# First expert products over 240 token columns instead of 256

## The chip, the core and the metric

The kernel runs on one core of a Trainium2 chip. The metric is the device time of one launch in microseconds (us), taken as the median of several runs. The engines of the core are named as the profile names them: PE is the matrix engine (PEld its weight loads), DVE the vector engine, ACT the scalar engine, POOL the GpSimd engine, and SP issues most transfers.

## What is computed

Three layers follow each other. A linear attention with a decaying state gives 3072 rows `x` of 384 numbers. A first layer of eight experts sends each row that a skip score lets through to one expert and adds the gated result. A second layer mixes all rows into 32 slots, four for each of eight other experts, and spreads the outcome over the rows again. The change lies in the first expert layer:

```
for e in range(8):
    mask = e_idx == e
    h = np.maximum(xc[mask] @ w1[e], 0.0)          # w1[e]: 384 x 1024
    y[mask] = gate_w[mask, None] * (h @ w2[e])     # w2[e]: 1024 x 384
out[do_compute] = xc + y
```

How many rows an expert gets depends on the data. For the inputs that `setup_inputs` draws with seed 0 the fullest expert has 205 rows; with seeds 1 to 7 the fullest has 240.

## The kernel before

The rows of one expert are gathered into a block with room for `CAP = 256` tokens, two halves of 128. Places that no token takes hold zeros or are masked later. `gload(e)` fetches the block from DRAM by an index list on POOL, `gtr(e, ...)` turns it on PE, and ACT and DVE write it as a rounded high part and a rounded rest, `xh` and `xl` (tile `xhl` in the profile), 128 x 3 x 256 each. The matrix products of this layer are made in the rounded four-byte type `F32R`; to keep four-byte accuracy each product is three: high by high, low by high, high by low.

The layer is a loop over `n` from 0 to 31, four steps for each expert; one step takes 256 of the 1024 inner features. In one step stand, in this order:

- `mm1(n)`: the first product, with weights as the stationary side (128 x 128 pieces of `wa`) and tokens as the moving side, 256 columns. There are six pieces (three of the 384 inputs by two of the features) and three products for each, so 18 products a step: L1251, L1252 and L1254, all into the PSUM tile `hp`.
- `split`: ACT rounds the next pieces of weights (L1007) and DVE makes their rests (L995).
- `act(n)`: ACT takes the positive part of `hp` into `hh` (L1261), and DVE makes the rest `hlo` (L1262). Both tiles are 128 x 2 x 256, two buffers each, taken anew from a pool in every step.
- `mm2(n-1)`: the second product of the step before, with 128 tokens of `hh` or `hlo` as the stationary side and 384 columns of weights as the moving side: 12 products, L1276 to L1278, into `yp`.
- between these, pieces of the work around the experts: `fin_a` adds the gated outcome to the rows (L1284 on DVE), `fin_b` to `fin_d` make the logits of the second layer, `gtr` turns the block of the next expert, `wload` fetches weights three half experts ahead (L957, L959), and `vload` fetches weights of the second layer (L200).

The order of PE, DVE, ACT and POOL is written out by hand: they run the program in the order of the code. SP follows the same order in this part; at the end of the program stands a read of the flag `bad` into a register on every engine (L1587), and on SP the scheduler puts that read where it likes after the flag is written.

The flag is written in step `n == 2` by four small DVE operations (L1383 to L1388) out of the counts of rows. Where an expert has more than 256 rows, a second program, `general`, computes everything again after the fast one. After the loop come the second layer's experts (`experts`: L214, L223, L232) and the mixing into the output (`combine`: L297 to L304).

Of the kernel before, what the change touches and what calls it, by code (L numbers as in the profile page):

```python
# [8 lines left out]
F32 = mybir.dt.float32  # L9
F32R = mybir.dt.float32r  # L10
BF16 = mybir.dt.bfloat16
I32 = mybir.dt.int32
AF = mybir.ActivationFunctionType
ALU = mybir.AluOpType
# [5 lines left out]
P = 128  # L20
# [3 lines left out]
E = 8  # L24
F = 1024
CAP = 256
XW = DM + 1
NOROW = 65536
NEG = -1.0e30
# [442 lines left out]
def tile_main(ctx, tc, rk, kv, wu, wcat, phi, w1, w2, v1, v2, r_in, k_in, v_in, w_in, u_in, wcn, out, dbg=None, force=False):  # L472
    nc = tc.nc
# [79 lines left out]
    cn = {"ident": ident, "onesf": onesf, "sel4": sel4, "w8": w8}  # L553
    x = xp.tile([P, NT, XW], F32, name="x")
    tj_i = kp.tile([P, 2, NT], I32, name="tj_i")
# [32 lines left out]
    n = 1  # L588
# [175 lines left out]
    tok8 = ry.tile([P, 2 * B, 16], BF16, tag="tok8", bufs=1, name="tok8")  # L764
    hot8 = ry.tile([P, 2 * B, CAP], BF16, tag="hot8", bufs=1, name="hot8")
    ipl = ry.tile([P, CAP], F32, tag="ipl", bufs=1, name="ipl")
    selb = rt.tile([P, E], BF16, tag="selb", bufs=1, name="selb")
# [14 lines left out]
    def hots(g, bs, eng):  # L782

        j0, nb = GR[g]
        if g < 4 and g not in HOT:
            HOT[g] = hot8[:, B:] if g % 2 else ry.tile([P, B, CAP], BF16, tag="hot", bufs=1, name=f"hot{g}")
        for b in bs:
# [3 lines left out]
    def gathered(g):  # L791

        li = ps.tile([P, CAP], F32, tag="t", name=f"lip{g}")
        for b in range(B):
            nc.tensor.matmul(li[32 * b : 32 * b + 32, :], tok[g % 2][:, b, :], HOT[g][:, b, :], start=True, stop=True)
        LI.append(ry.tile([P, CAP], BF16, tag="li", name=f"li{g}"))
        nc.scalar.copy(LI[g], li)
# [216 lines left out]
    if True:  # L1014
        for i in range(NT):
# [89 lines left out]
            if i == 4:  # L1105
# [6 lines left out]
                nc.vector.tensor_sub(tj[:, 1], tf[:, 1], tj[:, 0])  # L1112
                nc.gpsimd.iota(ipl.bitcast(I32), pattern=[[E, CAP]], base=-NOROW, channel_multiplier=0)
                nc.gpsimd.tensor_copy(ipl, ipl.bitcast(I32))
# [14 lines left out]
        fs = rt.tile([P, E], BF16, tag="fs", bufs=1, name="fs")  # L1129
# [39 lines left out]
        hl = fst.enter_context(tc.tile_pool(name="hl", bufs=1))  # L1169
        cw = hst.enter_context(tc.tile_pool(name="cw", bufs=2))  # L1170
# [10 lines left out]
        def gates_of(e):  # L1181
            for bl in range(2):
                fetched(XT[e][3][:, bl : bl + 1], g_d, e, bl)

        def fetched(o, src, e, bl):
            nc.gpsimd.indirect_dma_start(  # L1186
                out=o, out_offset=None, in_=src,
                in_offset=bass.IndirectOffsetOnAxis(ap=idg[:, bl, e : e + 1], axis=0),
                bounds_check=B * S - 1, oob_is_err=False,
            )  # L1190
# [4 lines left out]
        nc.vector.scalar_tensor_tensor(ltm[:, 16:24, :], m8.to_broadcast([P, 8, 32]), NEG, lg8[:, :, 9:41], op0=ALU.mult, op1=ALU.add)  # L1195
        nc.vector.tensor_reduce(cmax2, ltm[:, 16:24, :].rearrange("t b s -> t s b"), axis=AX.X, op=ALU.max)
        nc.gpsimd.tensor_copy(lt[:, 16:24, :], lg8[:, :, 9:41])
        gates_of(0)
        gates_of(1)
        gv = Group("v", cmax2, ltm[:, 16:24, :], 8, lambda j: x[:, 16 + j], lx[:, 1:2, :], mcs[:, 1:2])  # L1200
# [43 lines left out]
    def mm1(n):  # L1244
        xh, xl = XT[n // 4][1:3]
        hi, lo = WS.pop(("a", n))
        hp = pc.tile([P, 2, CAP], F32, tag="hp", name=f"hp{n}")

        fk = [(f, k, slice(f * P, f * P + P)) for k in range(3) for f in range(2)]
        for f, k, fs in fk:  # L1250
            nc.tensor.matmul(hp[:, f, :], hi[:, k, fs], xh[:, k, :], start=(k == 0 and f == 0), stop=False)  # L1251
            nc.tensor.matmul(hp[:, f, :], lo[:, k, fs], xh[:, k, :], start=False, stop=False)  # L1252
        for f, k, fs in fk:
            nc.tensor.matmul(hp[:, f, :], hi[:, k, fs], xl[:, k, :], start=False, stop=(k == 2 and f == 1))  # L1254
        HH[n] = [hp]

    def act(n):
        hp = HH[n][0]
        hh = cw.tile([P, 2, CAP], F32R, tag="hh", bufs=2, name=f"hh{n}")
        hlo = cw.tile([P, 2, CAP], F32R, tag="hlo", bufs=2, name=f"hlo{n}")  # L1260
        nc.scalar.activation(hh, hp, AF.Relu)  # L1261
        nc.vector.scalar_tensor_tensor(hlo, hp, 0.0, hh.bitcast(F32), op0=ALU.max, op1=ALU.subtract)  # L1262
        HH[n] = (hh, hlo)

    def mm2(n):
# [74 lines left out]
    if True:  # L1340
# [4 lines left out]
        for n in range(NS + 1):  # L1345
# [5 lines left out]
            if n < NS:  # L1351
                mm1(n)
                if 1 < n + 1 < NS and n > 0:
                    split("a", n + 1)
                if n > 1:
                    split("b", n)
                act(n)
            f = e - 1
# [22 lines left out]
            if n == 2:  # L1381
                mxc = mk.tile([P, 1], F32, name="mxc")
                nc.vector.tensor_reduce(mxc, cnt[:, 0:E].rearrange("p e o -> p (e o)"), axis=AX.X, op=ALU.max)  # L1383
                okc = mk.tile([P, 1], F32, name="okc")
                nc.vector.tensor_scalar(okc, mxc, float(E * CAP), None, op0=ALU.is_le)
                okw = mk.tile([P, 1], F32, name="okw")
                nc.vector.scalar_tensor_tensor(okw, cnt[:, E, :], float(E * PR), okc, op0=ALU.is_equal, op1=ALU.mult)
                nc.vector.tensor_scalar(bad, okw[0:1], -1.0, 1.0, op0=ALU.mult, op1=ALU.add)  # L1388
# [38 lines left out]
            if n == 23:  # L1427
                for i, o in enumerate((0, 1536)):
                    k = next(vit)
                    V[k] = vload(nc, XV, f"xv{i}", 1, k, v1, v2)  # L1430
            if n == 4:
                k = next(vit)
# [7 lines left out]
            if n % 2 == 1 and 3 <= n < 3 + 2 * NVX:  # L1440
                k = next(vit)
                V[k] = vload(nc, vx, "vx", NVX, k, v1, v2)
            if n % 2 == 1 and n // 2 + 3 >= 2 * E:
                for _ in range(2 if n < NS - 1 else 1):
                    k = next(vit)
# [49 lines left out]
        nm = mk2.tile([32, 1], F32, name="nm")  # L1495
# [159 lines left out]
```

## Time and profile before

| | us |
|---|---|
| median of three runs | 358.16 |
| the three runs | 357.42, 358.16, 359.10 |
| the profiled execution | 355.71 |
| its span, first to last instruction | 354.0 |

| engine | busy us | share of the span |
|---|---|---|
| PE | 326.0 | 92% |
| PEld | 261.7 | 74% |
| DVE | 230.9 | 65% |
| ACT | 160.8 | 45% |
| POOL | 141.7 | 40% |

The busy time of PE adds the whole length of products that overlap in its pipeline, with modelled ends, so a busy PE is not a PE at its peak. What one product costs in a dense row is read from the distance between two starts, and what an engine loses from the rows on waiting. The chain of work that ended last holds a single row in this profile (the read of the flag on ACT) and tells nothing here, so the stages are read one by one.

### The profile page before, as it was taken

What the parts mean: (1) busy time and instruction counts of PE and PEld (TensorE: products, weight loads), DVE (VectorE), ACT (ScalarE), POOL (GpSimd) and SP (SyncE); (2) the same over time, 40 slices, a digit from 0 to 9 for tenths busy, and PEclk for the clock granted to TensorE, in tenths of its full rate; (3) what the DMA queues carried; (4) which work ended last, traced back from release to release, by engine and by line L of the source; (5) the groups of instructions that cost most, each with busy time, mean ns of one, the idle gap of its engine ahead of it and who ended that gap; (6) DMA issues with size and microseconds to landing.
All of it is one profiled execution on the core that took longest, in us unless ns stands there. A gap on an engine that the chain in (4) does not pass through costs nothing. (4 is left out here: it accounts for less than half of the span.)

```text
span 354.0 us, 10396 instructions
## 1 busy us (share of the span) xinstructions
PE 326.0 (92%) x4316; PEld 261.7 (74%) x4316; DVE 230.9 (65%) x510; ACT 160.8 (45%) x351; POOL 141.7 (40%) x179
## 2 busy tenths in 40 slices
PE   8888998899798998999999999999999999999750
PEld 3556775777676683999999999998999998734340
DVE  6658678786878737776674847665575846417650
ACT  2234553445344554554655546554654643221360
POOL 4737775676655564814323242525224102200000
PEclk9999999999999999999999999999999999999985
DMA  7956568576678955789788787778856639489396
GB/s 243 312 166 187 148 196 277 176 215 190 201 214 277 386 211 182 269 269 317 263 275 284 241 266 258 252 271 270 306 179 224 221 107 329 156 270 372 119 328 214
DMA packets 45735, 85.29 MB, mean 241 GB/s; under 512 B 3838, under 2 KB 26672, under 8 KB 45680
## 3 DMA queue, kind: packets, MB, share of 16 engines
q1 hardware_dynamic: 43024, 80.63, 68.5%
q0 software_dynamic: 2128, 3.74, 3.7%
q8 instruction: 36, 0.59, 0.7%
q10 hardware_dynamic: 528, 0.16, 0.2%
q14 instruction: 19, 0.16, 0.2%
HBM read 74.49 MB, written 10.10 MB: 239 GB/s over the span
## 5 line engine op out<-in xcount | busy, mean ns | idle before, releaser
L1251 PE MATMUL hp<-xhl,wa 128*128 128x256 f32 x192 | 48.5, 289 | 0.2 <-ACT xhl L1241 0.2
L1252 PE MATMUL hp<-xhl,wa 128*128 128x256 f32 x192 | 47.1, 282 | 0.0
L1276 PE MATMUL yp<-wb,hh 128*128 128x384 f32 x128 | 45.1, 352 | 0.0
L995 DVE TENSOR_TENSOR wa<-w,wa 128x768 fp32r<-128x768 f32 x32 | 30.5, 956 | 22.0 <-ACT wa L1007 22.0
L1278 PE MATMUL yp<-wb,hlo 128*128 128x384 f32 x128 | 42.9, 335 | 0.0
L1277 PE MATMUL yp<-wb,hh 128*128 128x384 f32 x128 | 42.8, 335 | 0.0
L629 POOL TENSOR_TENSOR pd<-rkb 112x512 f32<-112x512 f32 x24 | 30.6, 1273 | 27.8 <-PE ud L657 23.4
L1186 POOL DMA_INDIRECT xg<-x_d,idg x16 | 19.9, 1242 | 52.1 <-DVE x L1284 39.4
L1306 POOL DMA_INDIRECT lt_d<-lsr,ids x16 | 17.7, 1106 | 52.5 <-ACT xhl L1241 29.9
L1251 PEld LDWEIGHTS hp<-xhl,wa 128*128 128x128 f32 x192 | 36.4, 190 | 0.5 <-ACT xhl L1241 0.5
L1252 PEld LDWEIGHTS hp<-xhl,wa 128*128 128x128 f32 x192 | 36.5, 190 | 0.0
L744 PE MATMUL yp<-at,kvt 64*48 64x64 f32 (+3 forms) x800 | 26.4, 248 | 7.2 <-DVE at L705 6.8
L995 DVE TENSOR_TENSOR wb<-w,wb 128x768 fp32r<-128x768 f32 x32 | 30.6, 955 | 2.4 <-ACT wb L1007 2.2
L744 PEld LDWEIGHTS yp<-at,kvt 64*48 64x48 f32 (+1 forms) x800 | 20.0, 120 | 15.0 <-DVE at L705 9.6
L705 DVE COPY_PREDICATED at<-ih,ud 128x512 f32<-128x512 int32 x24 | 17.4, 726 | 20.8 <-ACT us L686 8.7
L1261 ACT ACTIVATE hh<-hp 128x512 fp32r<-128x512 f32 x32 | 19.1, 598 | 26.0 <-PE hp L1254 26.0
L1007 ACT CAST wb<-w 128x768 fp32r<-128x768 f32 x32 | 26.8, 837 | 8.8 <-PE yp L1278 5.0
L1262 DVE SCALAR_TENSOR_TENSOR hlo<-hp,hh 128x512 fp32r<-128x512 f32 x32 | 22.0, 688 | 12.4 <-ACT hh L1261 12.4
L1254 PE MATMUL hp<-xhl,wa 128*128 128x256 f32 x192 | 28.2, 283 | 0.0
L1007 ACT CAST wa<-w 128x768 fp32r<-128x768 f32 x32 | 26.9, 840 | 0.0
L1276 PEld LDWEIGHTS yp<-wb,hh 128*128 128x128 f32 x128 | 24.1, 188 | 3.5 <-issue 3.5
L1254 PEld LDWEIGHTS hp<-xhl,wa 128*128 128x128 f32 x192 | 25.3, 192 | 0.0
(344 smaller groups left out, 693.3 us busy)
## 6 DMA issues: line engine op xcount, KB each, us to landing
w<-in_w_dram SPq DMA_DIRECT2D x32, 768.0 KB, 5.5
v<-in_v_dram SPq DMA_DIRECT2D x29, 768.0 KB, 6.8
rkb<-in_rk_dram SPq DMA_DIRECT2D x24, 448.0 KB, 5.6
kvt<-in_kv_dram SPq DMA_DIRECT2D x24, 384.0 KB, 3.7
x_d<-x SPq DMA_DIRECT2D x5, 768.0 KB, 6.5
out_dram<-ob SPq DMA_DIRECT2D x5, 768.0 KB, 6.8
x<-in_v_dram SPq DMA_DIRECT2D x2, 768.0 KB, 5.9
x_d<-x SPq DMA_DIRECT2D x2, 384.0 KB, 2.9
```

The lines of the kernel that those rows point to most:

```text
L629: nc.gpsimd.tensor_mul(t["pd"], rkt[:, 0], rkt[:, 1])
L744: nc.tensor.matmul(d, kvt[s0 : s0 + HT, 1, h * D : h * D + m], w, start=(c == ph == z == 0), stop=(ph == z == 1))
L995: nc.vector.tensor_sub(lv, sl, hv.bitcast(F32))
L1007: nc.scalar.copy(hv, sl)
L1186: nc.gpsimd.indirect_dma_start(out=o, out_offset=None, in_=src, in_offset=bass.IndirectOffsetOnAxis(ap=idg[:, bl, e : e + 1], axis=0), bou ...
L1251: nc.tensor.matmul(hp[:, f, :], hi[:, k, fs], xh[:, k, :], start=(k == 0 and f == 0), stop=False)
L1252: nc.tensor.matmul(hp[:, f, :], lo[:, k, fs], xh[:, k, :], start=False, stop=False)
L1254: nc.tensor.matmul(hp[:, f, :], hi[:, k, fs], xl[:, k, :], start=False, stop=(k == 2 and f == 1))
L1262: nc.vector.scalar_tensor_tensor(hlo, hp, 0.0, hh.bitcast(F32), op0=ALU.max, op1=ALU.subtract)
L1276: nc.tensor.matmul(YP[e][bl], hh[:, f, bs], hi[:, f, :], start=st, stop=False)
L1277: nc.tensor.matmul(YP[e][bl], hh[:, f, bs], lo[:, f, :], start=False, stop=False)
L1278: nc.tensor.matmul(YP[e][bl], hlo[:, f, bs], hi[:, f, :], start=False, stop=en)
```

## The change

`mm1` streams 240 token columns instead of 256, and writes 240 of the 256 columns of `hp`. `act` reads and writes 2 x 240 columns instead of 2 x 256. `hh` and its rest (now `hl`) are no longer taken anew from a pool in every step: two fixed pairs are made ahead of the loop, used in turn, and the last 16 columns of each half are set to zero once by four operations on POOL. `mm2` is unchanged; it reads all 256 columns, and so takes the zeros. The flag now asks for more than 240 rows.

```diff
+ROOM = 240
...
         nc.gpsimd.tensor_copy(lt[:, 16:24, :], lg8[:, :, 9:41])
+        HB = [[cw.tile([P, 2, CAP], F32R, tag=f"h{nm}{i}", bufs=1, name=f"h{nm}{i}") for nm in "hl"] for i in range(2)]
+        for ts in HB:
+            for t in ts:
+                nc.gpsimd.memset(t[:, :, ROOM:CAP].bitcast(F32), 0.0)
         gates_of(0)
         gates_of(1)
...
-            nc.tensor.matmul(hp[:, f, :], hi[:, k, fs], xh[:, k, :], start=(k == 0 and f == 0), stop=False)
-            nc.tensor.matmul(hp[:, f, :], lo[:, k, fs], xh[:, k, :], start=False, stop=False)
+            nc.tensor.matmul(hp[:, f, 0:ROOM], hi[:, k, fs], xh[:, k, 0:ROOM], start=(k == 0 and f == 0), stop=False)
+            nc.tensor.matmul(hp[:, f, 0:ROOM], lo[:, k, fs], xh[:, k, 0:ROOM], start=False, stop=False)
         for f, k, fs in fk:
-            nc.tensor.matmul(hp[:, f, :], hi[:, k, fs], xl[:, k, :], start=False, stop=(k == 2 and f == 1))
+            nc.tensor.matmul(hp[:, f, 0:ROOM], hi[:, k, fs], xl[:, k, 0:ROOM], start=False, stop=(k == 2 and f == 1))
...
-        hh = cw.tile([P, 2, CAP], F32R, tag="hh", bufs=2, name=f"hh{n}")
-        hlo = cw.tile([P, 2, CAP], F32R, tag="hlo", bufs=2, name=f"hlo{n}")
-        nc.scalar.activation(hh, hp, AF.Relu)
-        nc.vector.scalar_tensor_tensor(hlo, hp, 0.0, hh.bitcast(F32), op0=ALU.max, op1=ALU.subtract)
+        hh, hlo = HB[n % 2]
+        h, l, p = (t[:, :, 0:ROOM] for t in (hh, hlo, hp))
+        nc.scalar.activation(h, p, AF.Relu)
+        nc.vector.scalar_tensor_tensor(l, p, 0.0, h.bitcast(F32), op0=ALU.max, op1=ALU.subtract)
...
-                nc.vector.tensor_scalar(okc, mxc, float(E * CAP), None, op0=ALU.is_le)
+                nc.vector.tensor_scalar(okc, mxc, float(E * ROOM), None, op0=ALU.is_le)
```

PE has the same number of rows in the same order before and after; the 576 products of `mm1` have another width. POOL has four rows more, ahead of the fetches of the gates of the first two experts. Before, on POOL, between the fetch of the first two blocks (`xg`) and the step that clears a column of the rows (`x`):

```order
L1186 DMA xg_2688<-x_d,idg 128x384 x2
L1197 COPY ltt<-lg_213 128x256
L1186 DMA gg_2680<-g_d,idg 128x1 x2
L1186 DMA gg_2689<-g_d,idg 128x1 x2
L1342 MEMSET x_2767 128x16
```

The same place after; `hh` and `hl` are the two fixed pairs:

```order
L1187 DMA xg_2688<-x_d,idg 128x384 x2
L1198 COPY ltt<-lg_213 128x256
L1202 MEMSET hh_2708 128x2x16
L1202 MEMSET hl_2709 128x2x16
L1202 MEMSET hh_2710 128x2x16
L1202 MEMSET hl_2711 128x2x16
L1187 DMA gg_2680<-g_d,idg 128x1 x2
L1187 DMA gg_2689<-g_d,idg 128x1 x2
L1347 MEMSET x_2775 128x16
```

So four fetches of gates stand behind four clearings. In `mm2` of the first two steps, the products that read the second half of `hh` and `hl` now wait for POOL; no other wait on PE, DVE or ACT in the loop is new.

On SP one thing moved. Before, at steps 4 to 7 (`w` and `v` are weights of the two layers):

```order
L200 DMA ltt<-in_v_dram 128x3x512
L957 DMA w_2_1_3118<-in_w_dram 128x3x512
L959 DMA w_2_1_3120<-in_w_dram 128x4x384
L200 DMA v_2_0_3122<-in_v_dram 128x3x512
L1587 TENSOR_LOAD bad
L1587 ISA x2
L957 DMA w_3_0_3240<-in_w_dram 128x3x512
```

After:

```order
L201 DMA ltt<-in_v_dram 128x3x512
L1592 TENSOR_LOAD bad
L1592 ISA x2
L958 DMA w_2_1_3114<-in_w_dram 128x3x512
L960 DMA w_2_1_3116<-in_w_dram 128x4x384
L201 DMA v_2_0_3118<-in_v_dram 128x3x512
L958 DMA w_3_0_3232<-in_w_dram 128x3x512
```

The read of the flag, which waits for DVE, went ahead of three transfers.

## Rows read from the trace of the kernel before

**Rows 1.** Busy time by stretch: us, then PE, PEld, DVE, ACT, POOL, clock, DMA.

```profile
162.00:301.00 139.00, 139.00 (x1017) 132.17 (x1016) 90.12 (x155) 73.35 (x142) 43.10 (x38) 1.00 0.76 253
```

**Rows 2.** Who waited for whom, 162 to 301 us: total, times, longest.

```profile
DVE wa L995 <- ACT wa L1007: 21.7, 14, 3.3
ACT hh L1261 <- PE hp L1254: 20.3, 26, 1.3
```

**Rows 3.** Timeline of PE in two steps: start us, length us, product.

```profile
236.24 0.28 PE L1251 MATMUL hp<-xhl,wa 128*128 128x256 f32 x1
...
237.67 0.88 PE L1254 MATMUL hp<-xhl,wa 128*128 128x256 f32 x6
...
239.02 0.33 PE L1276 MATMUL yp<-wb,hh 128*128 128x384 f32 x1
...
240.41 0.34 PE L1278 MATMUL yp<-wb,hlo 128*128 128x384 f32 x1
```

**Rows 4.** Products by line and shape, whole run: count, then busy us, mean ns.

```profile
L1251 PE MATMUL hp<-xhl,wa 128*128 128x256 f32 x192 | 48.5, 289 | 0.2 <-ACT xhl L1241 0.2
L1254 PE MATMUL hp<-xhl,wa 128*128 128x256 f32 x192 | 28.2, 283 | 0.0
L1277 PE MATMUL yp<-wb,hh 128*128 128x384 f32 x128 | 42.8, 335 | 0.0
L1298 PE MATMUL lgq<-x2t,ph 128*32 128x256 f32 x42 | 4.4, 391 | 0.0
L214 PE MATMUL ehp<-v,spx 128*32 128x512 f32 x78 | 10.9, 595 | 0.0
L1536 PE MATMUL s<-l,onesf 128*128 128x32 f32 x4 | 0.6, 276 | 0.0
```

**Rows 5.** Timeline of PE behind the loop: four narrow products in a row.

```profile
307.09 0.61 PE L1536 MATMUL s<-l,onesf 128*128 128x32 f32 x4
```

**Rows 6.** ACT and DVE, 162 to 301 us, by line and shape.

```profile
L1262 DVE SCALAR_TENSOR_TENSOR hlo<-hp,hh 128x512 fp32r<-128x512 f32 x28 | 19.2, 687 | 9.8 <-ACT hh L1261 9.8
L1242 DVE TENSOR_TENSOR xhl<-xtp,xhl 128x256 fp32r<-128x256 f32 x18 | 7.0, 418 | 1.1 <-ACT xhl L1241 0.7
L1261 ACT ACTIVATE hh<-hp 128x512 fp32r<-128x512 f32 x27 | 16.1, 598 | 20.3 <-PE hp L1254 20.3
L1241 ACT CAST xhl<-xtp 128x256 fp32r<-128x256 f32 x18 | 6.1, 379 | 0.0
```

**Rows 7.** Timelines of POOL, PE and DVE, start of the loop.

```profile
142.81 0.42 POOL L1197 COPY ltt<-lg 128x256 f32<-128x256 f32 x1
...
148.71 0.14 POOL L1342 MEMSET x<- 128x16 f32 x1
...
148.48 0.33 PE L1276 MATMUL yp<-wb,hh 128*128 128x384 f32 x1
...
162.50 1.20 DVE L1284 SCALAR_TENSOR_TENSOR x<-yp,gg,xg 128x384 f32<-128x384 f32 x2
```

**Rows 8.** Timelines of DVE and SP around the flag, and its read on SP (ns).

```profile
153.67 0.14 DVE L1388 TENSOR_SCALAR bad<-okw 1x1 int32<-1x1 f32 x1
...
152.11 0.48 SPq L200 DMA_DIRECT2D ltt<-in_v_dram  x1
157.16 0.37 SPq L957 DMA_DIRECT2D w<-in_w_dram  x1
...
L1587 SPq TENSOR_LOAD <-bad x1: 473/473/473, 160.7 to 160.7; - x1
```

**Rows 9.** Behind the loop: SP's last weight transfers, PE's wait, DMA by stretch.

```profile
310.43 10.34 SPq L200 DMA_DIRECT2D v<-in_v_dram  x8
...
332.46 0.85 PE L232 MATMUL sop<-v,x 128*32 128x384 f32 x8 [0.58 <-DMA v<-in_v_dram]
...
303.00:310.00 7.00, 7.00 (x60) 4.90 (x62) 2.31 (x13) 1.44 (x5) 2.36 (x3) 1.00 0.26 86
311.00:331.00 20.00, 20.00 (x204) 7.74 (x200) 10.97 (x27) 4.43 (x9) 0.59 (x1) 1.00 0.97 334
...
SPq L200 <- PE ehp L214: 12.3, 3, 10.6
```

## The prediction

> **What bounds the kernel now.** I first cut the span into stages and looked at the one that the change touches, the loop over the experts, from about 143 to 301 us; the row is its main part. In it PE has work in flight all the time, at a granted clock of 1.00, which is the 2.4 GHz level, while DVE is busy 90.12 of 139 us, ACT 73.35 and POOL 43.10, and the DMA engines 0.76 of the time [rows 1]. Second, the waits of that stretch: PE heads none of them. ACT waits 20.3 us in 26 pieces for the last product of `mm1`, and DVE waits 21.7 us for ACT [rows 2]. So the loop is as long as PE's queue of products, and what the change takes from PE there is taken from the loop. Third, since a busy PE counts overlapping products whole, I took the price of a product from the distances between starts [rows 3]. The twelve products from 236.24 to 237.67 are 1.43 us apart, 119 ns each; the six that follow take 0.88 us, and less the 283 ns of the last one [rows 4] that is 0.60 us for five, again 119 ns. The eight 384-column products from 239.02 to 240.41 stand 174 ns apart.
>
> **Part 1, 16 columns less in 576 products.** One hundred twenty-eight columns more cost 174 - 119 = 55 ns, or 0.43 ns a column. The mean lengths say the same in another way: 335 ns at 384 columns against 283 at 256 [rows 4], 0.41 ns a column. That is one column a cycle of the 2.4 GHz level. I take 0.41, so 16 columns are worth 6.6 ns. At 256 columns 256 x 0.41 = 105 ns of the 119 are columns, and some 13 ns come on top; at 384 columns the rest is 174 - 157 = 17 ns. So the distance at 240 columns should be 119 - 6.6 = 112 ns. The count is 3 x 192 = 576, of which [rows 4] shows two of the three lines (the middle one has as many): 576 x 6.6 ns = **3.8 us**.
>
> A product cannot follow another faster than its weights are loaded. Each of these products has its own 128 x 128 weights. The trace has a row of narrow products with weights of that size: four of 32 columns take 0.61 us in all [rows 5], the last 276 ns long [rows 4], so three distances fill 0.334 us, 111 ns each, although 32 columns at the 0.80 ns a column of plain f32 (worked out below) would fill only 26 ns. I read 111 ns as the floor that the weight load sets. The 112 ns that I expect lie just above it, so the floor should not bite; it would at some 238 columns. Because the first product of each of the 32 rows of 18 waits for something else and because the floor is so near, I take **3.6 us** from the 3.8. The bounds are 576 x (119 - 111) = 4.6 us, and nothing, if the 13 ns come on top of the floor too (a rival, below).
>
> The Trainium skill (TensorE: Matmul & The Clock Gate, sections "LDWEIGHTS" and "Back-to-back issue gap") puts a load of 128 columns at 107 ns and a product at its columns over 2.4 GHz plus 2.5 ns. By that the distance would be 109 ns at 256 columns and then the load's 107, a gain of 2.5 ns a product and 1.4 us in all. The measured 119 and 111 ns [rows 3 to 5] are both higher than the page's, and the gap between them is three times as wide, so the sum above goes by the rows.
>
> **Part 2, ACT and DVE.** `act` has 32 columns less on each. ACT takes 598 ns for 512 columns and 379 for 256, 0.86 ns a column; DVE 687 and 418, 1.05 [rows 6]. So 27 and 34 ns a step, 0.9 and 1.1 us in all. Both wait for PE in the loop [rows 2], so I count nothing. The two blocks are no longer contiguous; were that to cost more than it saves, the 20 us of ACT's waiting would cover it, and without that cover 100 ns more a step would be 3.2 us.
>
> **Part 3, the four clearings on POOL.** No row shows one of 128 x 32. The nearest is 0.14 us for 128 x 16 [rows 7]; four cost 0.6 us, 0.8 at most if they grow with size. They stand behind the copy that ends at 143.23 and would end at 144.0. Who waits: the four gate fetches behind them, whose first consumer is DVE at 162.50, and PE's first product on the second half of `hh`, which ran at 148.48 [rows 7]. There are 4 us of cover for PE and over 10 for the gates, so this costs nothing; without the cover, 0.6 us once.
>
> **Part 4, the read of the flag on SP.** It moves ahead of three transfers and waits there for DVE's flag. DVE wrote it at 153.67 + 0.14 us, SP's transfer before had been issued at 152.11, and the next was issued at 157.16 because it waited for DVE's use of a buffer, not for SP [rows 8]. The read takes 0.47 us and fits into the 3.3 us between. It costs nothing, and 0.5 us once without the cover.
>
> **Part 5, what follows the loop.** If the loop ends 3.6 us earlier, does the end move too? From 311 to 331 us the DMA engines are 0.97 busy with the last eight weight transfers, and PE waits 0.58 us for the last of them [rows 9]. That stretch is bound by transfers. But SP issues them from 310.43 on, after waiting 10.6 us for PE's first products of the second layer to free the buffers, and the DMA engines had little to do just before (0.26) [rows 9]. So the whole stretch is hung on PE and moves with it; nothing is late in its place. In the loop the same bytes go through in 2.3% less time, which takes the DMA share from 0.76 to 0.78.
>
> **Sum.** 355.71 us for the profiled execution less 3.6 gives 352.1. The median of the three runs stands 2.45 us higher, and I carry the difference over: 358.16 - 3.6 = **354.5 us**, 1.0% less.
>
> **Rivals.**
>
> *The weight load becomes the bound.* If a product needs the load and then the same 13 ns, 256 columns are already at the floor, the distance stays at 119 ns and the gain is nothing. For it: 111 and 119 ns are close, and PEld has a load in flight 132 of 139 us [rows 1]. Against it: at 384 columns, where the load is long hidden, the distance has as large a rest above its columns, so the rest belongs to the stream. It gives 357 to 358 us. The page's rule above, with its 1.4 us, gives 356.8 and belongs here.
>
> *The gain is lost at the end.* If the DMA engines in the loop could not follow and the last transfers landed as late as before, PE's wait of 0.58 us would grow to 4 and the time would stay at 358. The 0.26 just before the burst speaks against it.
>
> *A narrower product falls out of the fast way.* This is the case on the other side. Rounded products run one pair of load and product each (192 is 32 steps by six pieces); the plain f32 ones run as two pairs (L1298: seven experts by three is 21, and the row counts 42), and each pair streams at half the pace: 391 ns at 256 columns and 595 at 512 are 0.80 ns a column [rows 4]. Every rounded product in this trace has 256 or 384 columns, none has fewer, so no row shows that the fast way holds below 256. If 240 columns ran at the plain pace in one pair, each would cost 240 x 0.80 + 13 = 205 ns, 86 more, and 576 of them 50 us: 408 us. As two pairs each would cost 410, 291 more, 168 us in all: 526. Against it: the pace follows the type and not the width at all widths that the trace has, and the change keeps one product where there was one. It decides as soon as the first product of `mm1` stands more than 119 ns from the next.
>
> *A small loss.* The new waits and the fixed buffers tie a step to the one two before more tightly than I read, and PE waits 0.1 us in each step: 3.2 us, which eats the gain and leaves up to 361.
>
> **How the numbers follow.** The forecast has 0.64, with a range of its own from 353.3 (the 4.6 us bound, and a little of the spread of the runs) to 356.3. The weight load as bound has 0.16 and the loss at the end 0.05, both within half a per cent of no change. The narrower product off the fast way has 0.11, the small loss 0.04. Half a per cent, 1.8 us, is about what a measurement of this kernel can tell from no change, and the forecast of 3.6 us is twice that. Faster is 0.64, the same 0.21, slower 0.15. From 353.0 to 359.0 the forecast and the two cases without gain are held, 0.85 less some spread; the case above 400 is left out.
>
> **What would show it right or wrong.** In the profile of the changed kernel the twelve products of `mm1` ahead of the last six should stand 112 ns apart, and the mean length of L1254's successor should be 276 ns instead of 283. A distance still at 119 shows the weight load as the bound; above 119 shows the product off the fast way. The 384-column products should keep their 174 ns, the clock its 1.00, the loop should end 3.6 us earlier, SP's eight transfers should be issued near 306.8 instead of 310.43, and PE's wait for the last of them should stay near 0.6 us. The prediction is wrong if PE shows a wait for ACT, DVE or POOL in the loop, or if the loop gets shorter and the end does not.

## The result, and the profile after

The kernel with 240 columns takes 354.64 us (median of 14 runs) where the kernel before takes 358.63 us in the runs beside it (14 as well). The ratio is 0.989, with a 95% interval from 0.985 to 0.993; it leaves out the slower executions of both kernels, among them a single one of 1047 us before and one of 1697 us after, which no profile explains. It is faster by more than half a per cent, and the forecast was 354.5 us.

Executions of one and the same kernel differ by up to 7 us (349.74 to 356.60 us in six runs of the changed one), and in the two executions of it that are shown below the difference arises ahead of the loop over the experts; so the loop is compared by its own length, from the start of its first product into `hp` to the start of its last into `yp`, and the rest by what lies behind that. The execution first profiled after the change was such a late one, and the closer views below are of a second execution of the same kernel, called r240, beside which most of the experiments ran.

First the products of the execution after the change, grouped by line and shape (partitions x columns of the moving side, count, then busy us, mean ns of one, and idle time before them). They answer to [rows 4] and [rows 6]:

```profile
L1256 PE MATMUL hp<-xhl,wa 128*128 128x240 f32 x192 | 46.1, 282 | 0.2 <-ACT xhl L1246 0.2
...
L1257 PE MATMUL hp<-xhl,wa 128*128 128x240 f32 x192 | 44.6, 274 | 0.0
...
L1282 PE MATMUL yp<-wb,hh 128*128 128x384 f32 x128 | 43.0, 336 | 0.0
...
L1266 ACT ACTIVATE hh<-hp 128x480 fp32r<-128x480 f32 x32 | 18.3, 572 | 22.4 <-PE hp L1259 21.2
L1267 DVE SCALAR_TENSOR_TENSOR hl<-hp,hh 128x480 fp32r<-128x480 f32 x32 | 20.9, 654 | 9.7 <-ACT hh L1266 9.3
...
L1259 PE MATMUL hp<-xhl,wa 128*128 128x240 f32 x192 | 26.7, 275 | 0.0
```

The last line of `mm1` is 275 ns long on the mean and not 283 any more, the second product kept its 336 ns, ACT's step went from 598 to 572 ns and DVE's from 687 to 654. The idle time ahead of PE's rows is 0.2 us, at the start of the loop, and otherwise nothing.

Now the distances, which carry the prediction's sum. The timeline of PE in r240 (start us, length us, product), to be read against [rows 3]:

```profile
231.20 0.33 PE L1281 MATMUL yp<-wb,hh 128*128 128x384 f32 x1
...
232.59 0.33 PE L1283 MATMUL yp<-wb,hl 128*128 128x384 f32 x1
...
232.76 0.27 PE L1256 MATMUL hp<-xhl,wa 128*128 128x240 f32 x1
232.87 0.27 PE L1257 MATMUL hp<-xhl,wa 128*128 128x240 f32 x1
...
233.99 0.27 PE L1257 MATMUL hp<-xhl,wa 128*128 128x240 f32 x1
234.10 0.83 PE L1259 MATMUL hp<-xhl,wa 128*128 128x240 f32 x6
```

From 232.76 to 234.10 stand twelve products, 1.34 us or 112 ns each, where it was 119. The eight distances from 231.20 to 232.59 are 1.39 us, 174 ns each, as before.

The stretch that [rows 1] showed of before, in r240 (us, then busy time and count of PE, PEld, DVE, ACT and POOL, granted clock, DMA share, GB/s), and below it the waits from 160 to 296 us:

```profile
161.00:293.70 132.70, 132.70 (x995) 126.96 (x994) 87.15 (x147) 71.28 (x136) 43.17 (x38) 1.00 0.77 257
...
DVE wa L996 <- ACT wa L1008: 22.0, 14, 3.2
ACT hh L1266 <- PE hp L1259: 16.3, 20, 1.2
```

PE still has work in flight all the time, at 1.00, the level of 2.4 GHz. ACT's wait for the last product of `mm1`, 20.3 us before, is 16.3; DVE's wait for ACT is the same. PE heads no wait in this stretch.

The whole loop, and what follows it to the end of the span, in us:

| kernel | loop begins | loop ends | loop | behind it |
|---|---|---|---|---|
| before | 143.02 | 298.76 | 155.74 | 55.26 |
| after | 148.69 | 300.77 | 152.08 | 54.81 |
| r240, the same kernel | 141.91 | 293.67 | 151.76 | 54.95 |

The loop lost 3.7 us in one execution and 4.0 in the other, and the part behind it did not grow (it is 0.3 to 0.5 us shorter), so the end moved with the loop. The rows of r240 that answer to [rows 9]: SP's eight last weight transfers, PE's products on them, and SP's wait ahead of the transfers:

```profile
305.34 10.39 SPq L201 DMA_DIRECT2D v<-in_v_dram  x8
...
L233 PE MATMUL sop<-v,x 128*32 128x384 f32 x128 | 11.3, 489 | 0.6 <-DMA v<-in_v_dram 0.6
...
SPq L201 <- PE ehp L215: 12.3, 3, 10.6
```

SP issues them at 305.34 instead of 310.43, 5.09 us earlier, which is just how much earlier this loop ends (293.67 against 298.76). SP's wait for PE is 12.3 us as it was, and PE's wait for the last transfer still 0.6.

### The profile page after: what moved, and what is told of

Read it like the earlier page. It is cut to its first block, busy times and chain, and to the rows that moved or that the text cites. A ratio compares the mean times of both kernels' runs of the same rounds, so it can differ in the third digit from the quotient of the medians.

```text
span 355.6 us, 10401 instructions
## 1 busy us (share of the span) xinstructions
PE 326.7 (92%) x4316; PEld 261.8 (74%) x4316; DVE 228.0 (64%) x510; ACT 159.9 (45%) x351; POOL 142.7 (40%) x183
## 5 line engine op out<-in xcount | busy, mean ns | idle before, releaser
L1256 PE MATMUL hp<-xhl,wa 128*128 128x240 f32 x192 | 46.1, 282 | 0.2 <-ACT xhl L1246 0.2
L1257 PE MATMUL hp<-xhl,wa 128*128 128x240 f32 x192 | 44.6, 274 | 0.0
L1283 PE MATMUL yp<-wb,hl 128*128 128x384 f32 x128 | 43.0, 336 | 0.0
L1187 POOL DMA_INDIRECT xg<-x_d,idg x16 | 20.7, 1295 | 49.6 <-DVE x L1289 37.1
L1256 PEld LDWEIGHTS hp<-xhl,wa 128*128 128x128 f32 x192 | 36.3, 189 | 0.5 <-ACT xhl L1246 0.5
L1257 PEld LDWEIGHTS hp<-xhl,wa 128*128 128x128 f32 x192 | 36.2, 189 | 0.0
L745 PE MATMUL yp<-at,kvt 64*48 64x64 f32 (+3 forms) x800 | 27.7, 257 | 7.2 <-DVE at L706 6.8
L745 PEld LDWEIGHTS yp<-at,kvt 64*48 64x48 f32 (+1 forms) x800 | 21.3, 127 | 15.4 <-DVE at L706 9.5
L1266 ACT ACTIVATE hh<-hp 128x480 fp32r<-128x480 f32 x32 | 18.3, 572 | 22.4 <-PE hp L1259 21.2
L1267 DVE SCALAR_TENSOR_TENSOR hl<-hp,hh 128x480 fp32r<-128x480 f32 x32 | 20.9, 654 | 9.7 <-ACT hh L1266 9.3
L1259 PE MATMUL hp<-xhl,wa 128*128 128x240 f32 x192 | 26.7, 275 | 0.0
L1281 PEld LDWEIGHTS yp<-wb,hh 128*128 128x128 f32 x128 | 24.0, 188 | 3.6 <-issue 3.5
L1282 PEld LDWEIGHTS yp<-wb,hh 128*128 128x128 f32 x128 | 24.1, 188 | 0.0
```

The lines of the kernel that those rows point to most:

```text
L745: nc.tensor.matmul(d, kvt[s0 : s0 + HT, 1, h * D : h * D + m], w, start=(c == ph == z == 0), stop=(ph == z == 1))
L1187: nc.gpsimd.indirect_dma_start(out=o, out_offset=None, in_=src, in_offset=bass.IndirectOffsetOnAxis(ap=idg[:, bl, e : e + 1], axis=0), bou ...
L1256: nc.tensor.matmul(hp[:, f, 0:ROOM], hi[:, k, fs], xh[:, k, 0:ROOM], start=(k == 0 and f == 0), stop=False)
L1257: nc.tensor.matmul(hp[:, f, 0:ROOM], lo[:, k, fs], xh[:, k, 0:ROOM], start=False, stop=False)
L1259: nc.tensor.matmul(hp[:, f, 0:ROOM], hi[:, k, fs], xl[:, k, 0:ROOM], start=False, stop=(k == 2 and f == 1))
L1267: nc.vector.scalar_tensor_tensor(l, p, 0.0, h.bitcast(F32), op0=ALU.max, op1=ALU.subtract)
```

## The experiments

**The same kernel again, beside a kernel that has the fixed buffers but not the narrower product.** r240 is the changed kernel without an edit; fixed256 keeps the fixed pairs of buffers and the four clearings on POOL, and streams 256 columns:

```diff
-            nc.tensor.matmul(hp[:, f, 0:ROOM], hi[:, k, fs], xh[:, k, 0:ROOM], start=(k == 0 and f == 0), stop=False)
+            nc.tensor.matmul(hp[:, f, :], hi[:, k, fs], xh[:, k, :], start=(k == 0 and f == 0), stop=False)
...
-        h, l, p = (t[:, :, 0:ROOM] for t in (hh, hlo, hp))
+        h, l, p = hh, hlo, hp
...
-                nc.vector.tensor_scalar(okc, mxc, float(E * ROOM), None, op0=ALU.is_le)
+                nc.vector.tensor_scalar(okc, mxc, float(E * CAP), None, op0=ALU.is_le)
```

> The changed kernel again, on the chip of the next three runs. Theory of the prediction (the distance of two products is the larger of the weight load's 111 ns and 0.41 ns a column plus 13 ns): products of the first kind 112 ns apart, the loop over the experts (first product into hp to last into yp) 152.1 us long against 155.7 before, the stretch from there to the end as before (54.8 to 55.3 us); time 3 to 4 us below the kernel before. Rival (the gain is lost at the end): loop shorter, stretch behind it longer by as much.

> The change without its narrower products: the fixed pairs of hh and hl and the four clearings on POOL stay, but products, ACT and DVE work on all 256 columns, and the flag asks for 256. Theory (the gain is the columns' alone): products 119 ns apart, loop 155.7 us, within 0.3 us of the kernel before. Rival (fixed buffers tie a step to the one two before, or POOL's clearings hold PE): the loop up to 3.2 us longer, with PE waiting for ACT, DVE or POOL. Rival (the fixed buffers themselves bring a part of the gain): loop shorter than 155.4.

Measured: r240 took 352.95 us (6 runs) and fixed256 357.88 (12), where the kernel before took 358.04 (23). The ratios to it are 0.987 (0.977 to 0.997) and 1.002 (0.997 to 1.006). Two rows of fixed256 on PE (start us, length us), eight distances apart:

```profile
234.20 0.28 PE L1257 MATMUL hp<-xhl,wa 128*128 128x256 f32 x1
...
235.14 0.28 PE L1257 MATMUL hp<-xhl,wa 128*128 128x256 f32 x1
```

That is 0.94 us, 118 ns each, as in the kernel before; over the whole run the third line of `mm1` stands 120.0 ns apart in both. The loop is 155.75 us long, against 155.74. So the buffers and the clearings cost nothing together, and nothing is gained by them.

The read of the flag on SP, though, is not moved in fixed256. It stands behind the three transfers there, as in the kernel before:

```profile
162.69 0.50 SPq L201 DMA_DIRECT2D v<-in_v_dram  x1
...
L1592 SPq TENSOR_LOAD <-bad x1: 475/475/475, 163.2 to 163.2; - x1
```

So fixed256 says nothing on that move, and the traces of the two kernels have to settle it. These are all the waits that PE heads in the loop, before (143 to 299 us) and in r240 (142 to 296):

```profile
PE hp L1251 <- ACT xhl L1241: 0.2, 1, 0.2
...
PE hp L1256 <- ACT xhl L1246: 0.2, 1, 0.2
```

It is the same 0.2 us at the start of the loop, for ACT, with the read in either place; a transfer that SP issues earlier or later has no wait of PE to change. With that, all of the gain is in the width of the product.

**More columns and fewer.** One number is changed, in r248 and in r208:

```diff
-ROOM = 240
+ROOM = 248
```

```diff
-ROOM = 240
+ROOM = 208
```

> Room for 248 columns instead of 240, nothing else. Theory (columns plus 13 ns above a floor at 111): 0.41 x 248 + 13 = 115 to 116 ns, about half way between 112 and 119; the loop 1.8 to 2.1 us longer than with 240. Rival (a step between 240 and 256, for instance where the number of columns falls below 256): 112 ns and the loop of 240, or 119 ns and the loop of before.

> Room for 208 columns instead of 240, nothing else; the fullest expert of these inputs has 205 rows. Theory (weight load as floor): 0.41 x 208 + 13 = 98 ns lies below the floor, so the products stay 111 to 112 ns apart and the loop is within 0.5 us of that with 240. Rival (columns alone set the distance, no floor): 98 to 99 ns, the loop another 7.5 us shorter.

Measured: r248 took 355.65 us (10 runs, ratio 0.992, 0.987 to 0.997), r208 351.19 (6 runs, ratio 0.987, 0.977 to 0.996). The loops are 152.99 and 151.44 us long, against 151.76 with 240 columns. PE's timeline, two rows of r248 ten distances apart, then two of r208 eight apart:

```profile
232.65 0.27 PE L1257 MATMUL hp<-xhl,wa 128*128 128x248 f32 x1
...
233.80 0.28 PE L1257 MATMUL hp<-xhl,wa 128*128 128x248 f32 x1
```

```profile
232.59 0.27 PE L1257 MATMUL hp<-xhl,wa 128*128 128x208 f32 x1
...
233.48 0.27 PE L1257 MATMUL hp<-xhl,wa 128*128 128x208 f32 x1
```

With 248 columns it is 1.15 us by ten, 115 ns (114.0 and 114.7 on the mean of two lines over the run, a little less than the 115 to 116 expected, and the loop is 1.2 us longer than with 240 and not 1.8 to 2.1), and with 208 columns 0.89 us by eight, 111 ns. So from 256 to 240 columns the distance falls by 7 to 8 ns, and from 240 to 208, where the columns alone would be worth 13 ns, by one at most. A row by line and shape of r208 says the same: the mean length, which fell from 283 to 275 ns with the first 16 columns, falls no more.

```profile
L1259 PE MATMUL hp<-xhl,wa 128*128 128x208 f32 x192 | 26.8, 275 | 0.0
```

240 columns are at the floor of 111 to 112 ns, and a room for fewer tokens brings hardly more: the loop with 208 is 0.3 us shorter. The medians of r240 and r208 differ by more than that, but so do executions of one kernel, by what happens ahead of the loop.

**What the floor is.** If 111 ns is the load of 128 weight columns, fewer weight columns must lower it; if it is a fixed price of a pair of load and product, not. In m96n208 each piece of `wa` has 96 columns and the products 208, in m64n128 64 and 128. The edit of m96n208 against the changed kernel follows; cut from it are the same edit in the third line of `mm1`, clearings that cover the whole of the four tiles, and the flag, which asks for 256 again:

```diff
-ROOM = 240
+ROOM = 208
+WID = 96
...
-        fk = [(f, k, slice(f * P, f * P + P)) for k in range(3) for f in range(2)]
+        fk = [(f, k, slice(f * P, f * P + WID)) for k in range(3) for f in range(2)]
...
-            nc.tensor.matmul(hp[:, f, 0:ROOM], hi[:, k, fs], xh[:, k, 0:ROOM], start=(k == 0 and f == 0), stop=False)
+            nc.tensor.matmul(hp[0:WID, f, 0:ROOM], hi[:, k, fs], xh[:, k, 0:ROOM], start=(k == 0 and f == 0), stop=False)
...
-        h, l, p = (t[:, :, 0:ROOM] for t in (hh, hlo, hp))
+        h, l, p = (t[0:WID, :, 0:ROOM] for t in (hh, hlo, hp))
```

> Room for 208 columns and weights of only 96 of 128 columns in the first products: each piece of 128 inner features computes 96, and hh and its rest stay zero in the other 32 (a quarter of the expert's inner features is left out); as many products as before. Theory (the floor of 111 ns is the load of 128 weight columns): the load falls to 96/128 x 111 = 83 ns, so the columns set the distance again, 0.41 x 208 + 13 = 98 to 100 ns. Rival (111 ns is a fixed price of a product with its own weights): 111 to 112 ns as with 128 weight columns.

> Only 128 columns and weights of 64 columns in the first products (half of the tokens' room and half of the inner features are left out, hh and its rest stay zero there). Theory (the pace is one column a cycle at any width): the load falls to 56 ns, and the distance is 0.41 x 128 + 13 = 66 ns. Rival (a rounded product falls out of the fast way somewhere below 240 columns): 0.80 x 128 + 13 = 115 ns or more. Rival (111 ns is a fixed price of a product): 111 ns.

Measured: m96n208 took 348.58 us with a loop of 143.59, m64n128 335.51 with a loop of 132.00 (one run each, the kernel before 357.75). PE's timeline of m96n208, then of m64n128, each two rows eleven distances apart:

```profile
230.12 0.26 PE L1258 MATMUL hp<-xhl,wa 128*96 128x208 f32 x1
...
231.17 0.74 PE L1260 MATMUL hp<-xhl,wa 128*96 128x208 f32 x6
```

```profile
232.22 0.23 PE L1258 MATMUL hp<-xhl,wa 128*64 128x128 f32 x1
...
232.89 0.52 PE L1260 MATMUL hp<-xhl,wa 128*64 128x128 f32 x6
```

It is 1.05 us by eleven, 96 ns, in the one and 0.67 us by eleven, 61 ns, in the other. The same 208 columns that stood 111 ns apart behind 128 weight columns stand 96 ns apart behind 96. So the floor is set by the weight columns, and a fixed price of a pair is out. The rows of the loads themselves say the same. Here are the loads of one line of `mm1`, from 160 to 280 us, in r208, m96n208 and the two kernels of the next experiment (partitions x weight columns, count, then busy us, mean ns):

```profile
L1257 PEld LDWEIGHTS hp<-xhl,wa 128*128 128x128 f32 x150 | 28.7, 192 | 0.0
...
L1257 PEld LDWEIGHTS hp<-xhl,wa 128*96 128x96 f32 x156 | 25.2, 162 | 0.0
...
L1257 PEld LDWEIGHTS hp<-xhl,wa 128*64 128x64 f32 x149 | 20.0, 134 | 0.0
...
L1257 PEld LDWEIGHTS hp<-xhl,wa 128*32 128x32 f32 x161 | 17.6, 109 | 0.0
```

From 32 to 128 columns the length grows by 83 ns, or 0.86 ns a weight column (0.83 with the 189 ns of the same line in r240); 128 of them are 107 to 111 ns. The floor is also one of four-byte weights: in the kernel before, a row of 24 narrow products in `bf16`, each with a load of its own 128 x 128 weights, has 0.74 us less the 0.17 of the last one by 23, or 25 ns between starts:

```profile
132.42 0.74 PE L806 MATMUL idp<-tok,hot 128*128 128x8 bf16 x24
```

Products of 128 columns at 61 ns are also the clearest word on the narrow product: 128 columns fill 53 ns at 0.417 ns a column, so the pace holds at half the width, and nothing falls out of a fast way. The loop of m64n128 is no measure of this price any more, since PE there has work in flight for only 111.51 of 118 us:

```profile
160.00:278.00 118.00, 111.51 (x998) 104.47 (x998) 80.34 (x151) 65.61 (x138) 45.57 (x38) 0.99 0.88 297
```

61 ns was less than I had expected, and raised a new question: the prediction had 13 ns on top of the columns, and here there are 61 - 53, or 7 by the mean of 59.9 over the second and third line of `mm1` from 185 to 278 us, where the clock is 1.00.

**Is the price on top of the columns fixed?** m64n256 and m32n208 have the edit above with other numbers, so that neither is near its floor:

```diff
-ROOM = 240
+ROOM = 256
+WID = 64
```

```diff
-ROOM = 240
+ROOM = 208
+WID = 32
```

> Weights of 64 of 128 columns in the first products, all 256 token columns (half of the inner features is left out, hh and its rest stay zero there). Two readings of what a product costs above 0.417 ns a token column: a fixed 13 ns (seen at 128 weight columns) gives 106.7 + 13 = 119 to 120 ns; a part that grows with the weight columns (13 ns at 128, 10 at 96, 6 to 7 at 64) gives 113 ns.

> Weights of 32 of 128 columns in the first products, 208 token columns (three quarters of the inner features are left out, hh and its rest stay zero there). Fixed 13 ns above the token columns: 86.7 + 13 = 100 ns. A part that grows with the weight columns, 0.104 ns each: 86.7 + 3.3 = 90 ns.

Measured: m64n256 took 356.14 us with a loop of 152.91, m32n208 346.51 with a loop of 142.79 (one run each, the kernel before 358.60). PE's timeline, two rows seven distances apart in each:

```profile
234.25 0.28 PE L1258 MATMUL hp<-xhl,wa 128*64 128x256 f32 x1
...
235.06 0.28 PE L1257 MATMUL hp<-xhl,wa 128*64 128x256 f32 x1
```

```profile
233.16 0.26 PE L1258 MATMUL hp<-xhl,wa 128*32 128x208 f32 x1
...
233.84 0.26 PE L1257 MATMUL hp<-xhl,wa 128*32 128x208 f32 x1
```

The means over whole lines are steadier than these rows, which are rounded to 10 ns; for `mm1` they are taken over the second and third line, which have no first product of a row. That is 114.4 ns in m64n256, where the same 256 columns stand 119.4 apart behind 128 weight columns: nearer to the 113 of the part that grows than to the 119 to 120 of a fixed 13 ns, which is out. With 32 weight columns it is 96.3 ns, where a price that goes on falling with the weight columns would have given 90. The table sets the means beside the columns at 0.417 ns each (one a cycle of 2.4 GHz):

| weight columns | moving columns | distance ns | columns ns | on top ns |
|---|---|---|---|---|
| 128 | 384 | 174 | 160.0 | 14 |
| 128 | 256 | 119.4 | 106.7 | 13 |
| 96 | 208 | 96.6 | 86.7 | 10 |
| 64 | 256 | 114.4 | 106.7 | 8 |
| 64 | 128 | 59.9 | 53.3 | 7 |
| 32 | 208 | 96.3 | 86.7 | 10 |

Two pairs of rows differ in the weight columns (and so in the rows of `hp` that are filled) alone. At 256 moving columns the rest goes down from 13 to 8 ns when they go from 128 to 64; at 208 it is 10 ns behind 96 and behind 32. So the weight columns alone do not set the rest, and I have no run that says what else does.

## Why the prediction was right

**The bound (right).** The loop was as long as PE's queue, and a shorter queue made a shorter loop. Beyond 0.2 us at its start PE heads no wait in it before or after.

**Part 1, the products (right in sum, one step misread).** The distance fell to the forecast 112 ns, and the loop by 3.7 and 4.0 us where 3.6 was taken from 3.8. The mean distances make the longer of these two from the trace alone: in the first line of `mm1` 126.7 - 119.4 = 7.3 ns by 192, in the second 118.8 - 112.0 = 6.8 by 192, in the third 120.0 - 112.0 = 8.0 by the 161 distances within a row of products, 1.40 + 1.31 + 1.29 = 4.0 us. So a product gave 7 to 8 ns and not 6.6, since it stood at 119 to 120 and now stands at the floor. The forecast of 112 ns was met at the floor, then, and not by the price that it was worked out from; that the two lie within 1 ns of each other is in part luck.

The floor was also right: 111 ns read from three distances of narrow products [rows 5] was confirmed by r208 at 111. The step that failed, without harm, is "some 13 ns come on top" as a price of the stream that stays the same. The reason given, that 384 columns have as large a rest and so the rest belongs to the stream, falls with m64n256: the same 256 columns have 8 ns on top behind 64 weight columns. The price doesn't hold close to the floor either: 248 columns at 103.3 ns and 13 would be 116 ns and were 114. So the first eight columns gave 4 to 6 ns a product and the second eight 2 to 3, where a fixed price on top gives 3.3 for each. The loop shows the same: with 248 columns it is 1.2 us longer than r240's and 2.8 shorter than the kernel's before, and not half-way.

The Trainium skill (TensorE: Matmul & The Clock Gate, section "LDWEIGHTS") puts a load of 128 columns at 107 ns; r208 measures 111, and no line of `mm1` with 128 weight columns goes below 110 on the mean. Its rule that the load goes by columns, at 0.83 ns each, agrees with the 0.83 to 0.86 ns a weight column of the load rows above. What it has on top of the moving columns (2.5 ns, "Back-to-back issue gap", given there for an isolated product) is exceeded by every row of the table above, by 4 to 12 ns.

**Part 2, ACT and DVE (right).** 26 and 33 ns less a step (27 and 34 were expected), and nothing of it in the time: both still wait for PE. Fixed buffers cost nothing, which fixed256 shows.

**Part 3, the clearings (right, too dear).** POOL's timeline in r240, start us and length us:

```profile
141.92 0.41 POOL L1198 COPY ltt<-lg 128x256 f32<-128x256 f32 x1
142.27 0.13 POOL L1202 MEMSET hh<- 128x32 f32 x1
...
142.45 0.13 POOL L1202 MEMSET hl<- 128x32 f32 x1
142.74 1.03 POOL L1187 DMA_INDIRECT gg<-g_d,idg  x1 [0.16 <-issue]
```

Four stand 0.06 us apart, so they take 0.3 us and not 0.6: the rows overlap, and I had added their lengths up. The cover was wide enough for either.

**Part 4, the read on SP (right).** In r240 DVE wrote the flag at 152.10 us and SP read it right behind, ahead of its transfers:

```profile
152.10 0.14 DVE L1393 TENSOR_SCALAR bad<-okw 1x1 int32<-1x1 f32 x1
...
L1592 SPq TENSOR_LOAD <-bad x1: 462/462/462, 152.3 to 152.3; - x1
...
155.69 0.37 SPq L958 DMA_DIRECT2D w<-in_w_dram  x1
```

The read takes 0.46 us from 152.3 and the next transfer goes out at 155.69, so 2.9 us of the gap are left over. This rests on r240 alone, since fixed256 has the read where it was.

**Part 5, the end (right).** SP's eight transfers moved by the 5.09 us by which the loop's end did, and PE's wait for the last stayed at 0.6 us.

**The rivals.** "The weight load becomes the bound" is half true: it is the bound now, but at 111 to 112 ns and not at 119, so it cost only what could have been gained below 240. "The gain is lost at the end" falls with the table of the loops, and "a small loss" with fixed256 and with PE's 0.2 us of waiting in r240. "A narrower product falls out of the fast way" falls with the 112 ns at 240 columns and with the 60 ns at 128 (behind 64 weight columns).

## What to carry to other kernels

Price a change in the width of a product from distances between starts in a dense row, not from lengths. Look then in the same trace for the narrowest products with weights of the same size and of a type that loads as slowly (here plain `f32` did, and `bf16` would have misled by 86 ns): their distance is the floor, and it says how many columns are worth cutting (here to 240, and hardly any below). A change in an engine that is off the bound is worth pricing for what it covers. A kernel that has all of a change but its main edit settles these side costs at once, but see in its trace that it has them all: in fixed256 the order on SP had gone back to that of before.

## What the runs showed that I had not expected

**The price on top of the columns depends on the stationary side, but not on it alone.** At 256 moving columns it was 13 ns behind 128 weight columns and 8 behind 64; at 208 it was 10 behind both 96 and 32. What else it depends on stays open.

**The spread of whole runs is TensorE's clock ahead of the loop.** The stages ahead of the loop are the same in both kernels, but in the execution first profiled after the change two stretches ran at the level of 1.2 GHz (0.50). The row of the clock in 40 slices, of that execution, then that of r240:

```profile
PEclk9969997899999999999999999999999999999995
```

```profile
PEclk9999999999999999999999999999999999999995
```

The stretches of the first (us, busy time and count of PE, PEld, DVE, ACT and POOL, clock, DMA share, GB/s), and then the same 18 to 21 us in r240:

```profile
18.00:21.00 3.00, 0.90 (x8) 0.31 (x10) 1.72 (x3) 0.37 (x1) 0.65 (x1) 1.00 1.03 257
21.03:27.86 6.83, 6.83 (x104) 4.88 (x104) 2.39 (x4) 2.02 (x5) 2.26 (x2) 0.50 0.50 122
...
58.57:65.40 6.83, 6.83 (x115) 5.68 (x112) 4.60 (x10) 2.09 (x6) 3.38 (x5) 0.50 0.71 263
```

```profile
18.00:21.00 3.00, 2.15 (x31) 1.17 (x30) 0.83 (x2) 0.27 (x1) 0.26 (x1) 1.00 1.03 270
```

13.7 us at half the clock lose up to 6.8 us, and that loop began 6.8 us later than r240's (148.69 against 141.91). The times on record go with the clock as well: the changed kernel took 350.1 to 351.6 us where the mean granted clock of the launch was 0.987 or 0.988, and 356.2 to 357.6 us where it was 0.964 to 0.968. Ahead of the first fall PE had work for 0.90 of 3 us, and in r240, with the DMA engines as busy, it had work for 2.15 of the 3 and the clock stayed at 1.00. In r248 it was 0.46 of 3, and the clock fell at the same place. Whether a late transfer decides this from one execution to the next was not tried. An idle PE is not the whole of it: from 55.00 to 58.57 us PE was busy 2.13 us in the first execution and 2.12 in r248, and the clock fell behind that in the first alone.
